# Last w_out group of a token block: the order of the products over the accumulators, and two engines that copy them out

## The chip, the cores and the metric

One core of one Trainium2 chip runs the program. The metric is device time in microseconds, as the median of several executions. A separate execution was recorded by the hardware profiler, and every row below comes from that one.

## The reference

Attention within clusters, followed by two feed-forward layers. For each of 2 batches and 8 heads (768 positions, head size 64), queries and keys are assigned to the nearest of 16 centroids, and a query attends only to keys of its own cluster. The 1536 tokens of 512 features then pass two layers of the same form:

```python
def _moe_ref(x, w_in, w_out):            # first layer, SiLU
    h = x @ w_in
    g = h * (1.0 / (1.0 + np.exp(-h)))
    return (g @ w_out).astype(np.float32)

def _moe2_ref(x, w_in, w_out, alpha):    # second layer, PReLU
    h = x @ w_in
    g = np.maximum(h, 0.0) + alpha * np.minimum(h, 0.0)
    return (g @ w_out).astype(np.float32)
```

`w_in` is 512 x 2048, `w_out` 2048 x 512. Weights arrive as 8-byte floats and are converted on the chip.

## The kernel before

All matrices are kept as two float16 parts (a high part and the rest), so that a product takes three TensorE matmuls. Attention goes over 12 token tiles of 128 and 8 heads (96 units): scores (lines 796 and 800), a VectorE scaling with minimum (810), the exponential on ScalarE (815), the two parts (819, 820), a transposing DMA (826) and the product with the values (838). Beside it the weights are loaded (892) and converted (903 to 930), and tiles that are done pass the first layer (w_in products on line 1195, w_out products on line 1226).

The second layer goes over 3 token blocks of 512 tokens (`j` = 0 to 2). A block has 4 feature groups of 4 x 128 features. For a group, `plain_in` (block 0, products on line 1415) or `wino_in` (blocks 1 and 2, a Strassen-Winograd form, products on line 1439) makes the activations `g`, with VectorE on lines 1388 to 1400 and 1448 to 1450. `layer2_out` then multiplies them with `w_out` (line 1482) and adds into four PSUM accumulators of 128 x 512 float32, one for each tile of 128 tokens. The four are the halves of two PSUM tiles, and the tile names in the traces and orders below are those of these two:

```python
bank_s = [ps.tile([128, 2, 512], F32, tag=f"s{i}", name=f"s{i}") for i in range(2)]
acc = [bank_s[t // 2][:, t % 2] for t in range(4)]
```

Tiles t = 0 and 1 are in `s0` (also written `s_64`), tiles 2 and 3 in `s1` (`s_65`). After the last group of a block ScalarE copies the four out with a scale (line 1496), and SyncE's queue sends each to the output (line 1498).

The order in which instructions stand on each engine is not the order in which the code issues them. `plan_order` at the end takes all instructions, with dependencies that it works out for itself, and schedules them by list scheduling under costs written into the class `Plan`. In these dependencies a PSUM tile counts as one cell, and two reads of one PSUM tile by different instructions are kept in order as well. It does this once in program order and 60 times with priorities from the previous result plus noise, and keeps the one whose modelled end is earliest:

```python
noise = Random(4)
found = [self.run(list(range(len(self.ins))))]
for _ in range(rounds):
    back.run([noise.gauss(0, 0.1) - t for t in self.ended])
    found.append(self.run([noise.gauss(0, 0.1) - t for t in back.ended]))
return min(found, key=lambda x: x[0])
```

The noise is drawn instruction by instruction, in program order. Each engine runs its instructions strictly in the order that comes out, and the tile framework puts in the semaphore waits.

Of the kernel before, what the change touches and what calls it, by code (L numbers as in the profile page):

```python
# [11 lines left out]
F32 = mybir.dt.float32  # L12
# [4 lines left out]
ACTF = mybir.ActivationFunctionType  # L17
ALU = mybir.AluOpType
# [311 lines left out]
def cluster_attention_silu_prelu(  # L330
# [20 lines left out]
    nc = tc.nc  # L351
    B, H, S, D = q.shape
    C = centroids.shape[1]
    DM, DFF = w1_in.shape
    T = S // 128
# [5 lines left out]
    N2 = NTILE * 128 // NC2  # L361
# [7 lines left out]
    KB = 1024  # L369
# [7 lines left out]
    def view(off, dt, *dims):  # L377
        n = 1
        for d in dims:
            n *= d  # L380
        nb = n * (2 if dt in (F16, BF16) else 4)
        assert off % 4 == 0 and nb % 4 == 0 and off + nb <= total, (off, nb)
        a = arena[:, off // 4:(off + nb) // 4]
        if dt != F32:
            a = a.bitcast(dt)
        if len(dims) == 1:
            return a
        names = [f"a{i}" for i in range(len(dims))]
        pat = f"p ({' '.join(names)}) -> p {' '.join(names)}"
        return a.rearrange(pat, **{n: d for n, d in zip(names, dims)})  # L390
# [497 lines left out]
    def out_piece(o, j):  # L888
        return view(o + 4 * KB * j, F16, 2, 2, DM)
# [377 lines left out]
    slots = [o_xt + 4 * KB * ((len(chunks) + i) % 3) for i in range(3)]  # L1267
# [109 lines left out]
    def g_buf(n):  # L1377
        return view(o_w + (32 + 8 * (n % 4)) * KB, F16, 4, 2, N2)

    def features(n):  # L1380
        j, i = groups[n]
        if j == 0:
            return [4 * i + k for k in range(4)]
        return [2 * i, 2 * i + 1, 8 + 2 * i, 9 + 2 * i]
# [87 lines left out]
    def layer2_out(n):  # L1472
        j, i = groups[n]
        first, last = i == 0, i == KF // 4 - 1
        g = g_buf(n)
        acc = [bank_s[t // 2][:, t % 2] for t in range(4)]
        for q, f in enumerate(features(n)):
            wo = out_piece(o_w, f // 2)
            for t in range(4):
                k = 0  # L1480
                for a, bb in ((0, 0), (0, 1), (1, 0)):
                    nc.tensor.matmul(  # L1482
                        out=acc[t], lhsT=g[:, q, a, t * 128:(t + 1) * 128], rhs=wo[:, bb, f % 2],
                        start=(first and q == 0 and k == 0), stop=(last and q == 3 and k == 2),
                    )
                    k += 1
        if not last:
            return
        eo = l2[:, 6 + j:7 + j]
        nc.vector.tensor_scalar(  # L1490
            eo, l2[:, 2 + j:3 + j], w2["in"].inv_smin, w2["out"].inv, op0=ALU.mult, op1=ALU.mult
        )
        nc.vector.tensor_tensor(out=eo, in0=eo, in1=l2[:, 1:2], op=ALU.mult)
        for t in range(4):
            ob = view(slots[1 + t % 2] + 2 * KB * (t // 2), F32, DM)
            nc.scalar.activation(out=ob, in_=acc[t], func=ACTF.Copy, scale=eo)
            r = j * (N2 // 128) + t
            nc.sync.dma_start(
                out=out.rearrange("(b p t) d -> b t p d", b=B, t=T)[r // T, r % T], in_=ob
            )  # L1500


    att = attention()
# [55 lines left out]
    for n in range(len(groups) + OUT_LAG):  # L1559
        if n < NG:  # L1560
            plain_in(n)
            run_bg(NPC // 2)
        elif n < len(groups):
            wino_in(n)
        if n == NG - 1:
            for w in range(2):
                wino_ops(w)
            split_x2(1)
        if n == 2 * NG - 1:
            split_x2(2)  # L1570
        if n >= OUT_LAG:
            layer2_out(n - OUT_LAG)
# [33 lines left out]
```

## Time and profile before

| what | value |
|---|---|
| median of 3 executions | 745.43 us (744.39 to 745.95) |
| the profiled execution | 744.72 us |
| its span, first to last instruction | 742.9 us |
| TensorE (PE) busy | 661.5 us, 89% of the span |
| VectorE (DVE) busy | 596.1 us, 80% |
| ScalarE (ACT) busy | 480.3 us, 65% |
| GpSimd (POOL) busy | 123.9 us, 17% |
| mean granted TensorE clock | 0.963 of full speed |

Times are microseconds from the start of the span. A busy share is an average over stages that are limited by different engines. "L1482" is line 1482 of the kernel, `s<-arena` an instruction that reads SBUF and writes PSUM tile s0 or s1 (numbers are left out), and "idle before <-X" the time that an engine stood still until X released it.

### The profile page before, as it was taken

The numbers are of one execution on the slowest core, as the hardware profiler recorded it, in microseconds if no ns is written. First come the engines' busy times: TensorE is split into PE (matmuls) and PEld (weight loads), VectorE is DVE, ScalarE is ACT, GpSimd is POOL, SyncE is SP. The second block draws the span as 40 slices with busy tenths as digits, with TensorE's granted clock in tenths as the row PEclk, the third lists the DMA queues.
The fourth block names the chain that finished last, engine by engine and source line by source line (L and its number), as shares of the span: only waits on it lengthen the run. The fifth ranks groups of instructions, "written<-read, shape, count | busy, mean of one in ns | idle before, by whom it ended". The sixth has DMA issues, their size and how long they took to land.

```text
span 742.9 us, 16966 instructions
## 1 busy us (share of the span) xinstructions
PE 661.5 (89%) x7023; PEld 500.3 (67%) x7023; DVE 596.1 (80%) x1048; ACT 480.3 (65%) x763; POOL 123.9 (17%) x231
## 2 busy tenths in 40 slices
PE   0355568799999999999999999999999999999997
PEld 0244347679988888888887888864444776666643
DVE  4799999989789479778977755979999999966640
ACT  7996877978789559667866877977773622413111
POOL 4550231211324531121220010000000000000000
PEclk9995659999999999999999999999999999999999
DMA  7989999999999897998999934343200100001001
GB/s 227 306 217 299 265 257 168 169 196 164 191 160 202 139 183 132 171 173 146 160 157 137 273 106 140 115 170 119 109 1 0 57 2 1 1 1 58 1 0 57
DMA packets 237357, 100.86 MB, mean 136 GB/s; under 512 B 217312, under 2 KB 227552, under 8 KB 237280
## 3 DMA queue, kind: packets, MB, share of 16 engines
q1 hardware_dynamic: 237280, 99.78, 62.8%
q8 instruction: 55, 0.90, 0.5%
q14 instruction: 22, 0.18, 0.1%
HBM read 43.03 MB, written 3.15 MB: 62 GB/s over the span
## 4 chain that ended last, share of the span: by engine, by line
PE 43%; DVE 13%; DMA 6%; ACT 5%; issue 4%; POOL 2%; ACTq 0%; POOLq 0%; DVEq 0%
PE s L1482 11%; PE w L1195 9%; PE w L1226 7%; PE w L1439 4%; PE x L838 3%; DVE arena L930 3%; PE m L1439 2%; PE x L1439 2%; DMA arena<-in_moe_w_out_dram 2%; PE s L800 2%; PE s L796 2%; DMA arena<-in_moe_w_in_dram 2%; DMA arena<-arena 1%; DVE arena L917 1%; DVE arena L1305 1%
## 5 line engine op out<-in xcount | busy, mean ns | idle before, releaser
L1226 PE MATMUL w<-arena 128*128 128x256 f16 (+1 forms) x1296 | 154.8, 258 | 1.2 <-ACT arena L1233 0.9
L1195 PE MATMUL w<-arena 128*128 128x256 f16 (+1 forms) x1272 | 147.6, 256 | 1.0 <-DMA arena<-arena 0.5
L1482 PE MATMUL s<-arena 128*128 128x512 f16 x576 | 132.1, 379 | 1.7 <-DVE arena L930 1.3
L838 PE MATMUL x<-arena 128*128 128x64 f16 x1728 | 117.5, 197 | 13.3 <-DMA arena<-arena 13.3
L1226 PEld LDWEIGHTS <-arena 128*128 128x128 f16 x1344 | 111.6, 99 | 14.7 <-issue 1.4
L1195 PEld LDWEIGHTS <-arena 128*128 128x128 f16 x1344 | 110.8, 98 | 14.8 <-issue 2.0
L838 PEld LDWEIGHTS <-arena 128*128 128x128 f16 x1728 | 96.5, 101 | 26.8 <-DMA arena<-arena 16.9
L810 DVE TENSOR_SCALAR_CACHE_REDUCE s<-s,stat 128x768 f32<-128x768 f32 x96 | 97.9, 1022 | 20.4 <-PE s L800 18.6
L815 ACT ACTIVATE s<-s,stat 128x768 f32<-128x768 f32 x96 | 83.9, 874 | 43.0 <-DVE s L810 41.5
L820 DVE TENSOR_TENSOR arena<-s,arena 128x768 f16<-128x768 f32 x96 | 91.4, 953 | 13.1 <-ACT arena L819 12.9
L1482 PEld LDWEIGHTS <-arena 128*128 128x128 f16 x576 | 56.1, 98 | 64.0 <-issue 2.3
L819 ACT ACTIVATE arena<-s 128x768 f16<-128x768 f32 x96 | 77.3, 809 | 1.6 <-DMA arena<-arena 0.2
L1399 ACT ACTIVATE arena<-arena,stat 128x512 f16<-128x512 f32 x48 | 33.9, 718 | 67.5 <-DVE arena L1396 67.4
L1439 PEld LDWEIGHTS <-arena 128*128 128x128 f16 x672 | 65.7, 98 | 13.6 <-DVE arena L1450 0.3
L796 PE MATMUL s<-arena 80*128 80x384 f16 x192 | 67.6, 352 | 7.2 <-DVE arena L820 5.0
L800 PE MATMUL s<-arena 128*128 128x384 f16 x192 | 67.9, 354 | 0.0
L450 POOL TENSOR_SCALAR stat<-stat 128x1 int32<-128x1 int32 (+1 forms) x41 | 10.2, 249 | 339.7 <-DVE stat L445 239.8
L930 DVE SCALAR_TENSOR_TENSOR arena<-arena,stat 128x1024 f16<-128x1024 f32 x40 | 50.9, 1289 | 8.8 <-ACT arena L929 8.8
L929 ACT ACTIVATE arena<-arena,stat 128x1024 f16<-128x1024 f32 x40 | 46.0, 1173 | 16.6 <-POOL stat L450 4.8
L914 DVE SCALAR_TENSOR_TENSOR arena<-arena 128x1024 int32<-128x1024 int32 x32 | 39.3, 1227 | 17.6 <-ACT arena L907 17.5
L1439 PE MATMUL w<-arena 128*128 128x256 f16 x336 | 52.0, 273 | 0.0
L903 ACT ACTIVATE arena<-arena 128x1024 int32<-128x1024 uint32 x32 | 36.8, 1149 | 21.9 <-DMA arena<-in_moe_w_out_dram 11.8
(176 smaller groups left out, 1036.7 us busy)
## 6 DMA issues: line engine op xcount, KB each, us to landing
arena<-in_moe_w_in_dram SPq DMA_DIRECT2D x16, 1024.0 KB, 6.3
arena<-in_moe_w_out_dram SPq DMA_DIRECT2D x16, 1024.0 KB, 5.7
arena<-in_k_dram SPq DMA_DIRECT2D x8, 384.0 KB, 4.2
arena<-in_q_dram SPq DMA_DIRECT2D x6, 512.0 KB, 5.1
arena<-in_v_dram SPq DMA_DIRECT2D x8, 384.0 KB, 5.0
out_dram<-arena SPq DMA_DIRECT2D x12, 256.0 KB, 2.1
arena<-arena SPq DMA_TRANSPOSE x149, 4.3
arena<-in_centroids_dram SPq DMA_DIRECT2D x1, 32.0 KB, 3.1
```

The lines of the kernel that those rows point to most:

```text
L796: nc.tensor.matmul(out=sc[:, j, :hs], lhsT=qt2[0:D + C, h], rhs=kt2[0:D + C, h % 2, j * hs:(j + 1) * hs], start=True, stop=False,)
L800: nc.tensor.matmul(out=sc[:, j, :hs], lhsT=qt1[:, h], rhs=kt1[:, h % 2, j * hs:(j + 1) * hs], start=False, stop=True,)
L810: nc.vector.tensor_scalar(sc[:, :, :hs], sc[:, :, :hs], nd_cols[:, H * (n % 2) + h:H * (n % 2) + h + 1], None, op0=ALU.mult, op1=ALU.min, ...
L815: nc.scalar.activation(out=p, in_=p, func=ACTF.Exp, scale=-1.0, bias=bias, accum_out=sums[n % 2][:, h:h + 1])
L819: nc.scalar.activation(out=hl[:, 0], in_=p, func=ACTF.Copy)
L820: nc.vector.tensor_tensor(out=hl[:, 1], in0=p, in1=hl[:, 0], op=ALU.subtract)
L838: nc.tensor.matmul(out=x_ps[0][:, h], lhsT=pt[:, ph * T + t], rhs=vt[:, h % 2, t, vh], start=(i == 0), stop=(i == 3 * T - 1),)
L930: nc.vector.scalar_tensor_tensor(out=lo, in0=t, scalar=s, in1=hi, op0=ALU.mult, op1=ALU.subtract)
L1195: nc.tensor.matmul(out=hp[:, ff], lhsT=wi[:, a, kd], rhs=mov(bb, kd), start=(i == 0), stop=(i == 3 * KD - 1),)
L1226: nc.tensor.matmul(out=acc, lhsT=wo[:, a, f % 2, dt * 128:(dt + 1) * 128], rhs=g[:, f, bb], start=(i == 0), stop=(i == 3 * KF - 1),)
L1439: nc.tensor.matmul(out=hp[:, ff], lhsT=a_[:, a, kd, at + 128 * ff:at + 128 * ff + 128], rhs=b_[:, bb, kd], start=(k == 0), stop=(k == 5),)
L1482: nc.tensor.matmul(out=acc[t], lhsT=g[:, q, a, t * 128:(t + 1) * 128], rhs=wo[:, bb, f % 2], start=(first and q == 0 and k == 0), stop=(la ...
```

## The change

In the last group of a token block, the code issues the products of tiles 0 and 1 for all four features first, then their copies and output DMAs, and then the same for tiles 2 and 3. VectorE copies tiles 1 and 3, ScalarE tiles 0 and 2. In the other groups the products are issued as before, through the new inner function.

```diff
-        for q, f in enumerate(features(n)):
+        def products(q, f, ts):
             wo = out_piece(o_w, f // 2)
-            for t in range(4):
+            for t in ts:
                 k = 0
                 for a, bb in ((0, 0), (0, 1), (1, 0)):
                     nc.tensor.matmul(
...
         if not last:
+            for q, f in enumerate(features(n)):
+                products(q, f, range(4))
             return
...
-        for t in range(4):
-            ob = view(slots[1 + t % 2] + 2 * KB * (t // 2), F32, DM)
-            nc.scalar.activation(out=ob, in_=acc[t], func=ACTF.Copy, scale=eo)
...
+        for ts in ((0, 1), (2, 3)):
+            for q, f in enumerate(features(n)):
+                products(q, f, ts)
+            for t in ts:
+                ob = view(slots[1 + t % 2] + 2 * KB * (t // 2), F32, DM)
+                if t % 2:
+                    nc.vector.tensor_scalar(ob, acc[t], eo, None, op0=ALU.mult)
+                else:
+                    nc.scalar.activation(out=ob, in_=acc[t], func=ACTF.Copy, scale=eo)
+                r = j * (N2 // 128) + t
+                nc.sync.dma_start(
+                    out=out.rearrange("(b p t) d -> b t p d", b=B, t=T)[r // T, r % T], in_=ob
+                )
```

In the changed file the products are line 1483, the copies line 1506 (ScalarE) and 1504 (VectorE), and the DMA line 1508. The number of instructions is the same; six copies change the engine.

The end of the program on ScalarE stood so before, with the semaphores that each instruction waits for in brackets (PE_49 is TensorE's, Activation_49 ScalarE's, DMAHW a DMA queue's):

```order
559 L1458 ACTIVATE arena<-m,stat 128x512 [waits PE_49,Activation_49]
560 L1399 ACTIVATE arena<-arena,stat 128x2x256 [waits DVE_49] x4
561 L1496 ACTIVATE arena<-s_64,stat 128x512 [waits DMAHW1_49,PE_49,Activation_49]
562 L1496 ACTIVATE arena<-s_64,stat 128x512 [waits DMAHW2_49,Activation_49]
563 L1496 ACTIVATE arena<-s_65,stat 128x512 [waits DMAHW3_49,PE_49,Activation_49]
564 L1496 ACTIVATE arena<-s_65,stat 128x512 [waits DMAHW4_49,Activation_49]
```

Two of the four copies have left ScalarE, and stand at the end of VectorE's rows, which now are these:

```order
916 L1392 SCALAR_TENSOR_TENSOR arena<-arena,stat 128x512 [waits DVE_49]
917 L1396 SCALAR_TENSOR_TENSOR arena<-arena 128x512 [waits DVE_49] x2
918 L1400 SCALAR_TENSOR_TENSOR arena<-arena,stat 128x2x256 [waits Activation_49] x3
919 L1504 TENSOR_SCALAR arena<-s_64,stat 128x512 [waits DMAHW2_49,Activation_49]
920 L1504 TENSOR_SCALAR arena<-s_65,stat 128x512 [waits DMAHW4_49,Activation_49]
```

Both new rows wait for a DMA queue and for ScalarE's semaphore, and name no wait for TensorE; the ScalarE copies of tiles 0 and 2, which stay, wait for TensorE.

On TensorE the last product into `s0` before stands five products ahead of the end (rows 14036 of 14046, every second row a weight load):

```order
14034 L1482 MATMUL s0_64<-arena_70 128x512
14035 L1482 LDWEIGHTS arena_70
14036 L1482 MATMUL s0_64<-arena_70 128x512
14037 L1482 LDWEIGHTS arena_70
14038 L1482 MATMUL s1_65<-arena_70 128x512
```

In the changed kernel it stands 22 products ahead of the end, row 14046 again being the last:

```order
14000 L1483 MATMUL s1_65<-arena_70 128x512
14001 L1483 LDWEIGHTS arena_70
14002 L1483 MATMUL s0_64<-arena_70 128x512
14003 L1483 LDWEIGHTS arena_70
14004 L1483 MATMUL s1_65<-arena_70 128x512
```

Seventeen products into `s1` more now follow the last one into `s0`.

At the end of block 0 VectorE prepares the Winograd operands (1312 to 1316 with 930) and begins block 1 (1448, 1450). Before, the place read:

```order
751 L1316 SCALAR_TENSOR_TENSOR arena<-arena,stat 128x1024
752 L930 SCALAR_TENSOR_TENSOR arena<-arena,stat 128x1024
753 L1312 SCALAR_TENSOR_TENSOR arena<-arena,stat 128x1024
754 L930 SCALAR_TENSOR_TENSOR arena<-arena,stat 128x1024
755 L1312 SCALAR_TENSOR_TENSOR arena<-arena,stat 128x1024
756 L1448 TENSOR_TENSOR arena<-w_69,arena 128x512
757 L930 SCALAR_TENSOR_TENSOR arena<-arena,stat 128x1024
758 L1450 SCALAR_TENSOR_TENSOR arena<-m,stat,arena 128x512
```

Now it reads:

```order
750 L1316 SCALAR_TENSOR_TENSOR arena<-arena,stat 128x1024
751 L1342 SCALAR_TENSOR_TENSOR arena<-arena,stat 128x512
752 L1312 SCALAR_TENSOR_TENSOR arena<-arena,stat 128x1024
753 L1504 TENSOR_SCALAR arena<-s_64,stat 128x512
754 L1504 TENSOR_SCALAR arena<-s_65,stat 128x512
755 L930 SCALAR_TENSOR_TENSOR arena<-arena,stat 128x1024
756 L1448 TENSOR_TENSOR arena<-w_69,arena 128x512
757 L930 SCALAR_TENSOR_TENSOR arena<-arena,stat 128x1024
758 L1450 SCALAR_TENSOR_TENSOR arena<-m,stat,arena 128x512
```

Block 0's two VectorE copies stand next to each other ahead of the first 1448, and the second 1312 has moved to row 779. On TensorE, the last product of block 0 into `s1` now has 17 products of line 1439 ahead of it, where it had 65.

The order also differs far from the edit. On ScalarE near the start of the program, where the first keys (608, 636, 645) and the first weights (903, 907) are prepared, the rows before were:

```order
11 L903 ACTIVATE arena<-arena 128x1024
12 L608 ACTIVATE arena<-arena,stat 128x768 x2
13 L636 ACTIVATE arena<-arena 128x12x64
14 L907 ACTIVATE arena<-arena 128x1024
15 L636 ACTIVATE arena<-arena 128x12x64
```

They are now:

```order
11 L903 ACTIVATE arena<-arena 128x1024
12 L608 ACTIVATE arena<-arena,stat 128x768
13 L907 ACTIVATE arena<-arena 128x1024
14 L636 ACTIVATE arena<-arena 128x12x64
15 L608 ACTIVATE arena<-arena,stat 128x768
```

The weight conversion 907 has moved ahead of one 608 and one 636. VectorE's rows at the same place have the conversion 914 at row 31, ahead of the first row of the first one-hot (571); before, it stood at row 34, behind three of them.

## Rows read from the trace of the kernel before

**Rows 1.** The page: the clock granted in 40 equal slices, and PE's and VectorE's busy tenths.

```profile
PE   0355568799999999999999999999999999999997
...
DVE  4799999989789479778977755979999999966640
...
PEclk9995659999999999999999999999999999999999
```

**Rows 2.** Busy time by stage; the columns follow the second line of the group.

```profile
core 0: us, PE busy (x) PEld busy (x) DVE busy (x) ACT busy (x) POOL busy (x), PEclk, DMA share, GB/s
0.00:50.00 50.00, 13.70 (x174) 10.68 (x175) 34.81 (x86) 42.79 (x65) 25.90 (x59) 1.00 0.94 264
50.00:125.00 75.00, 46.74 (x536) 34.51 (x535) 69.76 (x136) 53.93 (x75) 15.79 (x24) 0.66 1.06 247
125.00:175.00 50.00, 44.16 (x776) 39.02 (x774) 44.75 (x78) 41.89 (x73) 11.83 (x20) 0.97 0.99 173
175.00:525.00 350.00, 345.89 (x4235) 288.45 (x4232) 278.78 (x511) 264.36 (x440) 68.88 (x123) 1.00 0.81 163
525.00:575.00 50.00, 47.98 (x235) 22.32 (x234) 50.00 (x61) 29.42 (x41) 1.12 (x4) 1.00 0.02 6
575.00:650.00 75.00, 74.93 (x551) 53.41 (x550) 74.71 (x117) 30.35 (x47) 0.34 (x2) 1.00 0.04 15
650.00:725.00 75.00, 75.00 (x473) 46.18 (x472) 43.26 (x67) 15.10 (x22) 0.00 (x0) 1.00 0.04 15
725.00:743.00 18.00, 13.12 (x61) 5.77 (x59) 0.00 (x0) 2.42 (x4) 0.00 (x0) 0.99 0.16 59
```

**Rows 3.** What PE waited for up to 165 us: total us, times, longest.

```profile
PE w L950 <- DVE arena L917: 18.9, 9, 5.6
PE x L838 <- DMA arena<-arena: 12.5, 8, 3.2
...
PE s L503 <- ACT arena L651: 7.0, 2, 6.3
```

**Rows 4.** The chain that ended last, three pieces of it: start, us, what.

```profile
592.77 1.75 PE w L1439 x16
...
735.97 2.17 PE s L1482 x10
...
738.29 0.69 ACT arena L1496
```

**Rows 5.** Instructions in order of time, 736.5 us to the end.

```profile
737.13 2.42 ACT L1496 ACTIVATE arena<-s,stat 128x512 f32<-128x512 f32 x4 [22.87 <-PE s L1482]
737.85 2.07 SPq L1498 DMA_DIRECT2D out_dram<-arena  x4
```

**Rows 6.** Lines 1496 and 1498: ns min/median/max, first and last start; DMA landing.

```profile
L1496 ACT ACTIVATE arena<-s,stat x12: 668/681/697, 582.9 to 738.9; 128x512 f32<-128x512 f32 x12
...
L1498 SPq DMA_DIRECT2D out_dram<-arena x12: 332/332/360, 583.6 to 739.6; - x12
...
DMA to landing us min/median/max: 2.0/2.1/2.3
```

**Rows 7.** Line 1388: VectorE reads 512 float32 columns of PSUM with a pointer scalar.

```profile
L1388 DVE TENSOR_SCALAR arena<-w,stat x8: 735/742/746, 499.7 to 544.2; 128x512 f32<-128x512 f32 x8
```

**Rows 8.** Instructions from 712 us: VectorE's 1400 takes over from ScalarE's 1399.

```profile
713.54 0.72 ACT L1399 ACTIVATE arena<-arena,stat 128x512 f16<-128x512 f32 x1 [2.45 <-DVE arena L1396]
714.29 0.75 DVE L1400 SCALAR_TENSOR_TENSOR arena<-arena,stat 128x512 f16<-128x512 f32 x1 [0.79 <-ACT arena L1399]
```

**Rows 9.** The end of block 0 on VectorE and ScalarE, in order of time.

```profile
579.87 0.74 DVE L1342 SCALAR_TENSOR_TENSOR arena<-arena,stat 128x512 f16<-128x512 f32 x1
...
582.92 1.28 DVE L1312 SCALAR_TENSOR_TENSOR arena<-arena,stat 128x1024 f32<-128x1024 f32 x1
...
586.51 0.68 DVE L1448 TENSOR_TENSOR arena<-w,arena 128x512 f32<-128x512 f32 x1
...
589.80 0.67 ACT L1496 ACTIVATE arena<-s,stat 128x512 f32<-128x512 f32 x1
```

More of the change, by code (lines that the diff above doesn't have):

```diff
@@ L1493, in layer2_out @@
         nc.vector.tensor_tensor(out=eo, in0=eo, in1=l2[:, 1:2], op=ALU.mult)
-        for t in range(4):
-            ob = view(slots[1 + t % 2] + 2 * KB * (t // 2), F32, DM)
-            nc.scalar.activation(out=ob, in_=acc[t], func=ACTF.Copy, scale=eo)
[L1497 to L1500, printed above, removed]
+        for ts in ((0, 1), (2, 3)):
[11 more added lines that the diff above has]
+                )
     att = attention()
```

## The prediction, made before the changed kernel had run

> **What bounds the kernel now.** I began with the page's busy tenths [rows 1]: PE stands at 9 from the eighth slice to the last but one, so from about 150 us on TensorE sets the pace. VectorE is at 9 in many slices too, so the question for each stage is who waits. The busy time by stage [rows 2] says it in us. Up to 175 us PE is busy 13.70 + 46.74 + 44.16 = 104.6 us and idle 70.4 us, and in the middle of that its granted clock is 0.66 on average, a mixture of the levels of 1.2 and 2.4 GHz. From 175 to 725 us it idles 4.11 + 2.02 + 0.07 + 0 = 6.2 us, at full clock. So the time is three parts: a start in which PE waits for conversions and transposes [rows 3], 550 us in which it hardly waits, and a tail. Of the tail, the chain that ended last [rows 4] shows that the last w_out product ends at 735.97 + 2.17 = 738.14 us; the remaining 4.8 us of the span are copies, the output DMA and the program's end.
>
> What can move the time is therefore the tail, a new wait of PE after 175 us, and anything that happens in the start.
>
> **The order of the products: 0 us.** In the planner's own dependencies a PSUM tile is one cell. Products into `s0` are a chain in the order of issue, feature by feature over tiles 0 and 1, and those into `s1` another. The new loops issue each chain in the same order as before; only their mixing in the program changes, and that mixing the planner chose freely before as well. The trace has it: the first copy starts at 737.13 us [rows 5], about 1.0 us ahead of the end of the last product, which is five products at 2.17 / 10 = 0.22 us each [rows 4], as many as the old order puts behind the last one into `s0`. Now 22 are behind it, so the copies of tiles 0 and 1 start some 4.8 us ahead of the end, but they were not what the end waited for: what ends last is `s1`. The number and kind of products stay.
>
> **The tail: +0.17 us.** Before, ScalarE copies tile 2 from 738.29 us [rows 4], and tile 3 starts at 738.9 us and takes 0.68 us [rows 6]: done at 739.58, last DMA issued at 739.6. The two copies overlap by a little, as start to start is 0.6 us. After, ScalarE copies tile 2 from 738.29 to 738.98. The new order shows VectorE's copy of tile 3 waiting for ScalarE's semaphore and naming none of TensorE: I read this as a wait for the ScalarE copy out of the same PSUM tile, so that the two do not run side by side. The hand-over costs 714.29 − (713.54 + 0.72) = 0.03 us [rows 8]; a VectorE read of 512 float32 columns of PSUM with a pointer scalar takes 0.74 us [rows 7]. So it ends at 738.98 + 0.03 + 0.74 = 739.75, and its DMA goes out at 739.77, 0.17 us later than before. Two DMAs instead of four are then near the end; landing takes 2.0 to 2.3 us [rows 6], so at best 0.3 us comes back. I take none: the last landing is that of one DMA either way. Bounds: −0.13 and +0.17 us.
>
> At this place a rule speaks against my reading. The Trainium skill, "PSUM — Partial Sum Buffer", section Specifications (TRN2), says that ScalarE and VectorE can read PSUM in parallel at full bandwidth where they are not in the same bank; tiles 2 and 3 are 2 KiB per partition each, thus two of its banks. By that rule nothing in the chip keeps the copies apart. No run here shows two such reads together yet, and the wait is one that the program makes.
>
> **The ends of blocks 0 and 1: 0 us.** VectorE gets two copies of 0.74 us in each. At block 1's end PE is busy 75.00 of 75 us and VectorE only 43.26 [rows 2], so 1.5 us vanish in its slack. At block 0's end VectorE has no slack: 74.71 of 75 us [rows 2]. There the old order has six instructions from 1342 to the first 1448, 579.87 to 586.51 us, 6.64 us [rows 9]. The new order takes out a 1312 and the 930 that follows (1.20 us each, by the pitch of 582.92 to 586.51, which is three such) and puts in two copies: 6.64 − 2.40 + 1.48 = 5.72 us, and the first 1448 could come 0.9 us early. Against this stands the wait of the second copy. It needs ScalarE's copy of tile 2, which started at 589.80 before [rows 9]. On TensorE the last `s1` product has moved ahead of 48 Winograd products of 1.75 / 16 = 0.11 us [rows 4], so it can start at about 584.6 and end at 585.2. VectorE wants its second copy after 1342, 1316, 1312 and the first copy, at about 579.87 + 0.66 + 2.40 + 0.66 = 583.6. So it stands for up to 1.6 us, and the first 1448 comes between 0.9 us early and 0.7 us late. Behind it in VectorE's queue are 930 and 1450, for whose PSUM tile PE's next products wait. What hides it is PE's other work: from 575 to 650 us PE idles 0.07 us with VectorE full. Without that cover it is +0.7 us. I take 0.
>
> **The order elsewhere: 0 us, with wide bounds.** The noise is drawn in program order, and the program order has changed; the rows of the start show that another of the 61 orders has won. This touches 70.4 us of idle PE in the start and 6.2 us later. Both orders are the best of 61 under the same rules, so neither sign is preferred. As bounds I take the largest single wait of PE, 6.3 us [rows 3], gained or lost; for the likeliest case, within 1.5 us.
>
> **Sum.** 744.72 (profiled execution: span 742.9 and 1.8 around it) + 0 + 0.17 + 0 + 0 = 744.9 us. The profiled execution lies 0.71 us below the median of the runs, so against the median it is 745.43 + 0.17 = 745.6 us. A measurement of this kernel tells about 0.2% (1.5 us) from no change.
>
> **Rivals.**
>
> *Copies side by side.* If VectorE's wait is for an earlier instruction of ScalarE, the copy of tile 3 starts with that of tile 2 at 738.29 and ends at 739.03, 0.55 us earlier: 744.9 us. For it: the two halves are separate, by the rule above. Against: no wait for TensorE is named, and without the detour over ScalarE there would have to be one. No verdict hangs on it; it counts as no change.
>
> *The new order starts layer one sooner (faster).* The counted rows of the start show conversion (907, 914) ahead of key and one-hot work. PE waits 18.9 us for 917, conversion's last step, up to 5.6 us at a time, and 12.5 us for transposes, up to 3.2 us [rows 3]. If conversion comes a step sooner (one 917 of those nine waits, on average 2.1 us) and the products that it frees cover a transposing wait of 3.2 us, some 4 us are gained, allowing for overlap: 741.6 us. It decides from the point where PE's idle time before 175 us falls under 69 us.
>
> *The conversion delays the first attention units (slower).* The same rows read the other way. 914 ahead of the first 571 puts off the one-hot, its transpose, the first scores, and everything behind them in VectorE's queue, which is busy 69.76 of 75 us between 50 and 125 us [rows 2] and cannot catch up. And PE stands strictly in order: the wait of 6.3 us for 651 [rows 3] shows what one badly placed product costs. One more wait of half that size, 3.2 us, gives 748.8 us. It decides from the point where that idle time exceeds 72 us, or the clock stays at the lower level through more of 50 to 125 us: at 0.66 PE is busy 46.74 us there, at full clock the same work is 31 us, so a tenth more of this stage at the lower level is 1.5 to 2 us where PE is the one waited for.
>
> *VectorE falls behind at block 0's end (slower).* Priced above: +0.7 us, with the tail +0.9 us, 746.3 us. Alone it stays within 1.5 us; it matters only beside the rival before.
>
> **How the numbers follow.** Change without a measurable effect (my forecast, with side-by-side copies and block 0's delay in it): 0.40. Order faster by more than 1.5 us: 0.29. Order slower by more than 1.5 us: 0.31; a little over the faster one, as both direct terms are losses. The likeliest time is 745.6 us, its own range 744.1 to 747.1. The two outer cases reach 745.4 ∓ 6.3 us at the bounds; cutting a tenth off each side leaves 741.0 to 750.0.
>
> **What would show it.** Tail: VectorE's 1504 at the end begins 0.03 us after ScalarE's last 1506 has ended, and not with it; the last DMA is issued 1.6 us after the last product (now 739.6 − 738.14 = 1.5). Order of products: the first 1506 of block 2 starts some 4.8 us ahead of the last product, with nothing gained. Block 0: VectorE idle up to 1.6 us ahead of its second 1504, PE idle under 0.7 us more from 575 to 650. Order elsewhere: the difference in time, less 0.2 us, is that of PE's idle time up to 175 us and, by less, from 175 to 575. I am wrong if the tail shrinks by over 0.5 us, or if PE's idle time before 175 us moves by several us.

## The result, and the profile after

The changed kernel took 749.62 us (median of 6, 748.75 to 752.98) beside 745.07 us of the kernel before (median of 6, 744.39 to 749.38). The ratio is 1.0054 with an interval of 1.0035 to 1.0073: slower by half a per cent, 4.0 us by the ratio (the two medians are 4.55 us apart). The time lies inside the range forecast; "no change that can be measured" does not hold. The profiled execution of after is one of the six; at 752.28 us it is 2.7 us above the median of its kernel, so its 7.6 us of longer span (750.5 against 742.9) are more than the runs lost.

The page of after, the rows that answer to [rows 1]:

```profile
PE   0354567799899999999999998999999999999997
...
DVE  5799999978689589869976856779999999976640
...
PEclk9995558999999999999999999999999999999999
```

Two of TensorE's slices from the eleventh on stand at 8 where it had 9. Its busy time by stage, columns as in [rows 2]:

```profile
0.00:50.00 50.00, 13.21 (x163) 10.12 (x164) 34.53 (x85) 42.34 (x64) 26.27 (x55) 1.00 0.93 264
50.00:125.00 75.00, 48.97 (x580) 37.48 (x577) 70.29 (x134) 55.60 (x77) 14.87 (x28) 0.64 1.03 249
125.00:175.00 50.00, 43.47 (x760) 38.14 (x758) 44.57 (x79) 39.91 (x69) 11.86 (x19) 1.00 0.93 168
175.00:525.00 350.00, 341.34 (x4187) 285.25 (x4185) 268.58 (x500) 258.00 (x435) 70.85 (x124) 1.00 0.79 158
525.00:575.00 50.00, 47.83 (x230) 21.51 (x229) 49.69 (x62) 32.73 (x45) 1.31 (x4) 1.00 0.12 43
575.00:650.00 75.00, 74.34 (x529) 51.16 (x528) 75.00 (x110) 29.81 (x45) 0.78 (x2) 1.00 0.04 15
650.00:725.00 75.00, 74.87 (x499) 48.58 (x497) 54.01 (x88) 16.36 (x24) 0.00 (x0) 1.00 0.04 15
```

Up to 175 us PE is now busy 105.65 us and idle 69.35, 1.05 us less than before [rows 2]. From 175 to 525 us it is idle 350 − 341.34 = 8.66 us where it was 4.11, and from 575 to 650 us 0.66 where it was 0.07. What it waits for from 165 us on (total us, times, longest):

```profile
PE x L838 <- DMA arena<-arena: 3.3, 3, 2.0
PE s L503 <- ACT arena L944: 2.0, 4, 1.1
PE m L1195 <- DMA arena<-arena: 1.7, 1, 1.7
PE w L1226 <- ACT arena L1233: 0.9, 1, 0.9
PE m L1415 <- ACT arena L1233: 0.7, 1, 0.7
...
PE w L1439 <- DVE arena L1448: 0.7, 1, 0.7
```

No wait there is long. L838 waits for a transposing DMA of attention, L503 (a weight's sum of squares) for its conversion, L1195 for the transposed token tile, L1226 and L1415 for an eviction on ScalarE (L1233).

The tail answers to [rows 4, 5]. Two pieces of the chain that ended last, and then the instructions in order of time from 741 us:

```profile
734.79 11.24 PE s L1483 x52
...
746.10 0.70 ACT arena L1506
```

```profile
741.36 0.69 ACT L1506 ACTIVATE arena<-s,stat 128x512 f32<-128x512 f32 x1 [20.70 <-issue]
742.07 5.87 SPq L1508 DMA_DIRECT2D out_dram<-arena  x4
742.08 0.75 DVE L1504 TENSOR_SCALAR arena<-s,stat 128x512 f32<-128x512 f32 x1 [20.20 <-ACT arena L1506]
746.10 0.69 ACT L1506 ACTIVATE arena<-s,stat 128x512 f32<-128x512 f32 x1 [4.06 <-PE s L1483]
746.82 0.75 DVE L1504 TENSOR_SCALAR arena<-s,stat 128x512 f32<-128x512 f32 x1 [4.00 <-ACT arena L1506]
```

The last product ends at 734.79 + 11.24 = 746.03 us. VectorE's copy begins at 746.82, 0.03 us after ScalarE's has ended (746.10 + 0.69), and what released it was ScalarE. The line of the output DMAs, and their landing, for [rows 6]:

```profile
L1508 SPq DMA_DIRECT2D out_dram<-arena x12: 332/332/360, 585.8 to 747.6; - x12
...
DMA to landing us min/median/max: 2.0/2.0/2.1
```

### The profile page after: what moved, and what is told of

The parts are those of the page before. It is cut to its first block, busy times and chain, and to the rows that moved or that the text cites. A ratio compares the mean times of both kernels' runs of the same rounds, so it can differ in the third digit from the quotient of the medians.

```text
span 750.5 us, 16974 instructions
## 1 busy us (share of the span) xinstructions
PE 665.1 (89%) x7023; PEld 501.5 (67%) x7023; DVE 598.2 (80%) x1054; ACT 476.1 (63%) x757; POOL 125.9 (17%) x231
## 5 line engine op out<-in xcount | busy, mean ns | idle before, releaser
L1226 PE MATMUL w<-arena 128*128 128x256 f16 (+1 forms) x1296 | 148.5, 259 | 0.9 <-ACT arena L1233 0.9
L1195 PE MATMUL w<-arena 128*128 128x256 f16 (+1 forms) x1272 | 147.6, 257 | 0.7 <-DVE arena L1203 0.6
L1226 PEld LDWEIGHTS <-arena 128*128 128x128 f16 x1344 | 112.0, 99 | 13.8 <-issue 1.4
L838 PE MATMUL x<-arena 128*128 128x64 f16 x1728 | 110.6, 197 | 11.5 <-DMA arena<-arena 11.3
L1195 PEld LDWEIGHTS <-arena 128*128 128x128 f16 x1344 | 110.5, 98 | 15.0 <-issue 3.0
L838 PEld LDWEIGHTS <-arena 128*128 128x128 f16 x1728 | 92.2, 100 | 24.2 <-DMA arena<-arena 14.5
L1483 PEld LDWEIGHTS <-arena 128*128 128x128 f16 x576 | 56.1, 98 | 62.8 <-issue 0.7
L1439 PEld LDWEIGHTS <-arena 128*128 128x128 f16 x672 | 65.5, 98 | 14.4 <-issue 1.1
L450 POOL TENSOR_SCALAR stat<-stat 128x1 int32<-128x1 int32 (+1 forms) x41 | 12.5, 309 | 319.9 <-DVE stat L445 230.2
L930 DVE SCALAR_TENSOR_TENSOR arena<-arena,stat 128x1024 f16<-128x1024 f32 x40 | 51.6, 1305 | 7.6 <-ACT arena L929 7.5
L929 ACT ACTIVATE arena<-arena,stat 128x1024 f16<-128x1024 f32 x40 | 46.3, 1176 | 13.1 <-POOL stat L450 4.1
L1439 PE MATMUL w<-arena 128*128 128x256 f16 x336 | 49.5, 273 | 0.7 <-DVE arena L1448 0.7
```

The costliest lines, as they stand in the source:

```text
L838: nc.tensor.matmul(out=x_ps[0][:, h], lhsT=pt[:, ph * T + t], rhs=vt[:, h % 2, t, vh], start=(i == 0), stop=(i == 3 * T - 1),)
L930: nc.vector.scalar_tensor_tensor(out=lo, in0=t, scalar=s, in1=hi, op0=ALU.mult, op1=ALU.subtract)
L1195: nc.tensor.matmul(out=hp[:, ff], lhsT=wi[:, a, kd], rhs=mov(bb, kd), start=(i == 0), stop=(i == 3 * KD - 1),)
L1226: nc.tensor.matmul(out=acc, lhsT=wo[:, a, f % 2, dt * 128:(dt + 1) * 128], rhs=g[:, f, bb], start=(i == 0), stop=(i == 3 * KF - 1),)
L1439: nc.tensor.matmul(out=hp[:, ff], lhsT=a_[:, a, kd, at + 128 * ff:at + 128 * ff + 128], rhs=b_[:, bb, kd], start=(k == 0), stop=(k == 5),)
L1483: nc.tensor.matmul(out=acc[t], lhsT=g[:, q, a, t * 128:(t + 1) * 128], rhs=wo[:, bb, f % 2], start=(first and q == 0 and k == 0), stop=(la ...
```

## The experiments

All were timed beside runs of the kernel before on their own chip (its medians there were 747.69, 746.9 and 748.0 us), so a ratio is to be read within its batch. In kernels that change code above them, line numbers stand some 5 to 20 higher than in the kernel before. Expectations given in us go by the first batch, in which the kernel before took 745.07 us. "The old order" is that of the kernel before, "the new order" that of the changed kernel.

**Order or edit: four kernels.** In e1_old_order the planner is shown the program before (all copies priced as ScalarE's); after planning, the odd copies run on VectorE:

```diff
+            if t % 2:
+                moved.add(nc.vector.tensor_scalar(ob, acc[t], eo, None, op0=ALU.mult).ins.name)
+            else:
+                nc.scalar.activation(out=ob, in_=acc[t], func=ACTF.Copy, scale=eo)
...
+            if i.name in planned_as:
+                self.eng[n], self.cost[n], self.port[n] = 2, (0.19 + 512 / 1205.0 + 0.09,), False
```

> The planner is shown the old program (all copies as ScalarE's, old product loops), so that every engine keeps the old order; then the copies of tiles 1 and 3 are put on VectorE at the place where the plan had them begin. Theory 'order' (the 4.5 us come from the order that the planner chose for the changed program, not from the edit's own instructions): within 0.2% of before, 744.5 to 746.5 us. Rival 'edit' (VectorE's copies and their waits cost it, wherever the rest stands): near the changed kernel, 748.5 to 750 us.

Measured: 748.65 us, ratio 1.001 (0.999 to 1.003), so the edit in the old order can't be told from nothing. e2_new_order is the reverse: planned as the changed program, odd copies on ScalarE.

> The mirror: the planner is shown the changed program, so that every engine keeps the new order, and the copies of tiles 1 and 3 then run on ScalarE. Theory 'order': still as slow as the changed kernel, 748.5 to 750 us. Rival 'edit': back to 744.5 to 746.5 us.

Measured: 750.44 us, 1.0028 (1.0013 to 1.0044): the new order alone, with not one copy on VectorE, makes the kernel slower. It is half of the change's 1.0054, and less than this expectation gave (748.5 us is 1.0046 of 745.07); the interval overlaps a little with the change's (1.0035 to 1.0073). e3_loops has the new loops and all copies on ScalarE, e4_copies the old loops and odd copies on VectorE; e3_loops against the changed kernel:

```diff
-                if t % 2:
-                    nc.vector.tensor_scalar(ob, acc[t], eo, None, op0=ALU.mult)
-                else:
-                    nc.scalar.activation(out=ob, in_=acc[t], func=ACTF.Copy, scale=eo)
+                nc.scalar.activation(out=ob, in_=acc[t], func=ACTF.Copy, scale=eo)
```

> Only the product loops of the change, all copies on ScalarE. The order that the planner gives is almost the old one (1% of the rows of VectorE and ScalarE differ, around the ends of the blocks). Theory 'order': 744.5 to 746.5 us. Rival 'loops' (products tile by tile take PE's spare work away at the ends of blocks): 746.5 to 750 us.

> Only the VectorE copies of the change, product loops as before. The planner gives a third order, different from both. Theory 'order': any time of a spread of some us around the two known, 742 to 752 us, and with a lag that grows in stages that have no copies in them. Rival 'edit': 748.5 to 750 us, with the loss at the ends of the blocks.

Measured: e3_loops 746.97 us, 0.9992 (0.9976 to 1.0009); e4_copies 747.70 us, 0.9997 (0.9981 to 1.0014). The loops alone leave the order almost as it was. Of TensorE's 7,023 products, compared place by place with the kernel before, 22 come from another line of the program, against 2,774 with the whole change (691 of them up to 175 us, 1,992 from there to 525 us, 91 behind) and 3,012 with the copies alone. So what let another of the 61 orders win is the copies' move to VectorE, and the order that wins there with the old loops costs nothing.

**Where in the order: three kernels.** The changed kernel's instructions are planned twice, as the loops alone (old order) and as they are (new order), and the two are joined on every engine at one planned time, 500 us here and 210 us in new_start. In the traces TensorE's rows go over to the other order at about 518 and 219 us; the expectations say 512 and 223, which were estimates:

```diff
+    order = [
+        [n for n in x if begun[n] < 500.0] + [n for n in y if begun[n] >= 500.0]
+        for x, y in zip(one, two)
+    ]
```

> The changed kernel's instructions, in two orders joined: on every engine the old order (planned with all copies as ScalarE's, as in the kernel with the loops alone) up to the end of layer one, some 512 us, and the new order behind it. Theory (the new order loses its time in layer one, from 175 to 525 us, where TensorE stood 8.5 to 9.7 us in its four traces and 4.1 to 6.7 us in the old order's): at most 1.001 of before, TensorE idle 4 to 7 us from 175 to 525 us, and only the 0.7 us wait at the end of block 0 left. Rival (the loss lies in layer two and its copies): 1.003 to 1.006.

> The reverse: the new order on every engine up to some 512 us, the old one behind it. Theory (layer one): 1.003 to 1.006 of before, TensorE idle 8 to 10 us from 175 to 525 us and stopped near 455 us again. Rival (layer two): within 0.2% of before.

> The new order only up to some 223 us, the old one behind it. If the stop of 2 us near 195 us (L838 waits for a transposing DMA) is a part of the loss: 1.001 to 1.004 of before. If the loss of layer one lies behind it, at 375 to 520 us (weights and the last token tile late): within 0.2% of before, or a little faster, since the new order's start up to 175 us stood 1 us less.

Measured: old_then_new 748.05 us, 0.9999 (0.9982 to 1.0017); new_then_old 754.74 us, 1.0088 (1.0062 to 1.0114); new_start 747.95 us, 0.9994 (0.9972 to 1.0017). So the loss needs the new order between some 219 and 518 us, in layer one: with the old order there nothing is lost, and the new order only ahead of it costs nothing that can be measured. Behind the seam the two orders hardly differ on TensorE (the 91 products above). PE's waits from 375 to 650 us, first in old_then_new and then in new_then_old, show what goes and what stays:

```profile
PE w L1242 <- ACT arena L1249: 2.4, 1, 2.4
PE w L1455 <- DVE arena L1464: 0.7, 1, 0.7
```

```profile
PE m L1211 <- DMA arena<-arena: 2.5, 1, 2.5
PE s L518 <- ACT arena L960: 2.3, 2, 1.4
PE w L1431 <- DVE arena L1412: 2.0, 2, 1.5
```

With the old order up to the seam the waits for the token tile (L1195, here L1211) and the weight's sum of squares (L503, here L518) shrink to 0.5 us or vanish, while block 0's wait of 0.7 us for L1448 (here L1464) stays. The third row of new_then_old is new: those 2.0 us, at 524 and 528.7 us, are behind the seam, so I put about that much of its 1.0088 (above the 1.003 to 1.006 expected) down to the seam; no run shows it.

PE's idle time, window less busy, over all traces, with the time of the traced execution:

| kernel | order in layer one | traced execution | idle, 175 to 525 us | of it 375 to 525 us |
|---|---|---|---|---|
| before | old | 744.72 | 4.11 | 2.35 |
| e6_head_late | old, one product moved | 744.39 | 4.47 | 3.63 |
| e1_old_order | old | 751.98 | 5.96 | 3.91 |
| e3_loops | old | 748.15 | 6.65 | 4.23 |
| old_then_new | old | 748.23 | 5.67 | 3.05 |
| new_start | new to 219 us, then old | 750.69 | 6.93 | 4.26 |
| e4_copies | a third one | 747.76 | 5.83 | 5.51 |
| after | new | 752.28 | 8.66 | 5.57 |
| after_again | new | 756.91 | 9.68 | 6.75 |
| e2_new_order | new | 753.94 | 9.09 | 7.89 |
| e5_head_first | new, one tile moved | 751.91 | 8.54 | 7.48 |
| new_then_old | new | 753.85 | 8.70 | 7.71 |
| seed5 | another draw | 755.36 | 7.65 | 6.47 |
| seed6 | another draw | 757.93 | 11.40 | 8.53 |

The five with the old order in layer one average 5.37 us, the five with the new one 8.93 us, 3.6 us more. But these executions differ by more than the runs: they took 747.5 and 753.8 us on average, 6.3 us apart, since the traced ones of the new order lie 2.3 us above the medians of their kernels (the old ones 0.3 us). And idle time in layer one is not all that an order can lose: seed5 is 8 us slower than before with 3.5 us more of it.

**One late tile: three kernels.** after_again is the changed kernel once more.

> The changed kernel once more, beside the kernel before on this chip. Theory (the new order of the whole program costs the time): about 1.004 of before, inside 1.0035 to 1.0073, and its trace again shows TensorE standing for the transposing DMA of the last token tile ahead of the m products at L1195 near 455 us, 1.7 to 2.6 us, where the trace of before has no wait. Rival (the loss is a matter of single executions, in which a pause is or is not followed by a stretch at the lower clock): within 1.002 of before, and no wait near 455 us.

Measured: 751.75 us, 1.0074 (1.0046 to 1.0102), just above the range expected, with a stop of 2.1 us for the transposing DMA ahead of L1195. Where that stop comes from is seen by laying before and after side by side (instructions in order of time, before first):

```profile
436.34 1.20 ACT L929 ACTIVATE arena<-arena,stat 128x1024 f16<-128x1024 f32 x1
...
438.88 1.85 SPq L892 DMA_DIRECT2D arena<-in_moe_w_in_dram  x2
...
441.77 0.19 PE L838 MATMUL x<-arena 128*128 128x64 f16 x1
...
444.69 1.23 SPq L869 DMA_TRANSPOSE arena<-arena  x1
...
450.99 1.14 PE L1195 MATMUL m<-arena 128*128 128x256 f16 x9
...
451.97 0.19 PE L503 MATMUL s<-stat,arena 128*128 128x1 bf16 x2
```

```profile
444.36 1.22 ACT L929 ACTIVATE arena<-arena,stat 128x1024 f16<-128x1024 f32 x1 [3.01 <-POOL stat L450]
...
446.38 0.19 PE L838 MATMUL x<-arena 128*128 128x64 f16 x1
...
446.92 2.16 SPq L892 DMA_DIRECT2D arena<-in_moe_w_in_dram  x2
...
450.43 1.24 SPq L869 DMA_TRANSPOSE arena<-arena  x1
...
456.96 2.56 PE L1195 MATMUL m<-arena 128*128 128x256 f16 x22 [1.74 <-DMA arena<-arena]
...
459.70 0.19 PE L503 MATMUL s<-stat,arena 128*128 128x1 bf16 x2 [0.18 <-ACT arena L944]
```

The last attention products (L838) end the last token tile, which goes through VectorE and GpSimd to a transposing DMA (L869), and PE wants it at L1195. Before, that DMA is issued 5.8 us after two weight loads (L892) and PE never waits. After, loads and DMA are 3.5 us apart, and PE starts on the tile 6.5 us after the DMA's issue (450.43 to 456.96). The reader should also see the second chain: from the split of a weight piece on ScalarE (L929; when VectorE's L930 behind it has ended, the next load is issued) to the sum of squares of that next piece on PE (L503) it is 15.6 us before and 15.3 us after. Before, PE gets there without a wait.

e5_head_first lets the tile come sooner in the changed kernel:

```diff
+    pe[first - 40:first - 40] = head
...
+    dve.insert(at - 2, x)
...
+    sp.insert(at - 2, dma)
```

> The changed kernel in its own order, but the last 11 L838 products of the last token tile stand 40 products of L1226 (some 4.4 us) earlier on TensorE, VectorE's product of that tile two places earlier and its transposing DMA ahead of the two weight loads. Theory (the new order loses its time mostly where that tile comes late): no wait for the DMA ahead of L1195 near 455 us, and 2 to 3 us less than the changed kernel of the same batch, so about 1.001 of before. Rival (the loss is spread over the whole order, or is at the end of block 0): the wait goes and the time stays within 0.7 us of the changed kernel.

Measured: 750.68 us, 1.0053 (1.0035 to 1.0071), 1.07 us under after_again; the intervals overlap, so this decides for neither. The trace says more (order of time, this kernel's lines):

```profile
437.72 0.48 PE L855 MATMUL x<-arena 128*128 128x64 f16 x11
...
442.17 1.23 ACT L948 ACTIVATE arena<-arena,stat 128x1024 f16<-128x1024 f32 x1 [3.01 <-POOL stat L466]
...
444.11 1.23 SPq L888 DMA_TRANSPOSE arena<-arena  x1
445.43 1.32 SPq L911 DMA_DIRECT2D arena<-in_moe_w_in_dram  x2
...
452.56 2.56 PE L1214 MATMUL m<-arena 128*128 128x256 f16 x22
...
457.39 0.19 PE L519 MATMUL s<-stat,arena 128*128 128x1 bf16 x2 [2.27 <-ACT arena L963]
```

The wait for the tile is gone, and 4.8 us on PE stands 2.27 us for the weight piece instead. From the split (L948) to that sum of squares it is 15.2 us, as in after. Two chains were late by about as much, and shortening one uncovered the other.

e6_head_late moves a single instruction of the kernel before, the very last L838 product, 30 places back:

```diff
+    pe, n = order[0], place_of[last["products"][-1]]
+    at = pe.index(n)
+    pe.remove(n)
+    pe.insert(at + 30, n)
```

> The kernel before in its own order, but the very last L838 product stands 30 products of L1226 (some 3.3 us) later on TensorE; nothing else moves. Theory (that one tile's lateness is a price by itself): TensorE stands 1.1 to 3.5 us for the transposing DMA ahead of L1195 near 451 us, since the DMA landed at most some 2 us ahead of need in the trace of before; 1.0015 to 1.005 of before. Rival (later stages swallow such a wait, because VectorE sets the pace from 525 to 650 us): the wait is there and the time is within 0.2% of before.

```profile
443.14 0.19 PE L844 MATMUL x<-arena 128*128 128x64 f16 x1
...
446.93 1.23 SPq L877 DMA_TRANSPOSE arena<-arena  x1
...
450.02 1.14 PE L1203 MATMUL m<-arena 128*128 128x256 f16 x9 [0.77 <-DMA arena<-arena]
```

Measured: 747.04 us, 1.0003 (0.9986 to 1.002). The wait is 0.77 us, under the 1.1 to 3.5 us expected, and too small to settle anything by its time. But with the two loads issued 9.9 us earlier (436.99) the same transposing DMA needed 3.1 us from issue to PE's start (446.93 to 450.02), half of the 6.5 us in after. The other traces bear out that this goes with the place of the loads. The transposing DMA's time from issue to landing, by the time since the issue of the first of the two loads:

| issued | traces | landing after |
|---|---|---|
| 3.5 us behind the loads | after, after_again, e2_new_order, new_then_old | 6.5, 6.8, 7.3, 7.3 us |
| 3.8 us | e4_copies | 6.0 us |
| 5.8 us | before, e1_old_order, e3_loops, old_then_new | 4.4, 3.8, 4.2, 4.0 us |
| 9.9 us | e6_head_late | 3.0 us |
| 1.3 us ahead of them | e5_head_first | 3.0 us |

e5_head_first is the new order with this DMA moved ahead of the loads, and there it lands in 3.0 us. So in the new order the tile is late twice over: its products come later, and its DMA falls among the weight loads.

**Other draws: two kernels.** The kernel before with `Random(5)` and `Random(6)` in place of `Random(4)`:

```diff
-        noise = Random(4)
+        noise = Random(5)
```

> The kernel before with another seed for the noise of the planner's 60 further orders, nothing else changed. Theory (which order wins is as good as drawn, and orders differ by some tenths of a per cent): 0.995 to 1.010 of before, and nothing about it follows from the change. Rival (the planner's best orders are alike on the chip): within 0.2% of before.

> The kernel before with a third seed of the planner's noise. Theory (the winner of 61 orders is a draw on the chip): 0.996 to 1.011 of before, as likely slower than faster, and away from 1 by more than 0.2%. Rival (the first other seed was an exception): within 0.2% of before.

Measured: 754.96 us, 1.011 (1.0088 to 1.0132), and 756.27 us, 1.0117 (1.0087 to 1.0146). Two other draws, with nothing changed in the program, cost twice what the change cost. Both lie just above the ranges expected (1.010 and 1.011).

## Why the prediction was right or wrong

**The order of the products: right.** The first copy of block 2 starts at 741.36 us, 4.7 us ahead of the last product's end, and nothing is gained by it. With the loops alone the ratio is 0.9992 (0.9976 to 1.0009).

**The tail: right in its mechanism, small in both directions.** The copies out of one PSUM tile go one after the other, with the hand-over of 0.03 us that was forecast. The last DMA is issued 1.57 us after the last product (747.6 − 746.03; before 1.46), +0.11 for the +0.17 forecast. The span, though, ends 4.47 us after that product (750.5 − 746.03) instead of 4.76: 0.29 us are won at the end of the program, where I had taken none and allowed 0.13. This gain is the loops' and not the copies': the span ends 4.5 us after the last product in all eight traces with the new loops, two of which have every copy on ScalarE (e2_new_order, e3_loops), and 4.8 us after it in e1_old_order and e4_copies, which have VectorE's copies in the old loops. The rival with copies side by side falls. By the Trainium skill, "PSUM — Partial Sum Buffer", section Specifications (TRN2), different banks can be read by the two engines in parallel; the trace names a wait of the program (4.00 us, for ScalarE's L1506), and whether the chip would have read both banks at once no run here shows.

**The end of block 0: its price right, its cover not.** VectorE does not stand ahead of its second copy. ScalarE's copy of tile 2 has just ended when VectorE comes to its two copies (in order of time):

```profile
590.65 1.28 DVE L1312 SCALAR_TENSOR_TENSOR arena<-arena,stat 128x1024 f32<-128x1024 f32 x1
591.16 0.67 ACT L1506 ACTIVATE arena<-s,stat 128x512 f32<-128x512 f32 x1
591.84 1.40 DVE L1504 TENSOR_SCALAR arena<-s,stat 128x512 f32<-128x512 f32 x2
...
594.36 0.68 DVE L1448 TENSOR_TENSOR arena<-w,arena 128x512 f32<-128x512 f32 x1
...
595.09 1.91 PE L1439 MATMUL w<-arena 128*128 128x256 f16 x16 [0.66 <-DVE arena L1448]
```

VectorE is full (75.00 of 75 us), the two copies stand ahead of L1448, and PE stops 0.66 us for it. I had taken 0 because PE had other work; the upper bound of 0.7 us was about the value. That the copies are the cause, the other traces show: from 575 to 725 us PE is idle 0.00 to 0.15 us in the four with the old or new order and all copies on ScalarE (before, e2_new_order, e3_loops, e6_head_late), and 0.79 to 1.14 us in the eight with copies on VectorE. e2_new_order, which differs from the changed kernel in the copies' engine alone, has none of it. So the edit has a price of its own, some 0.7 to 1.1 us less the 0.3 us at the end, too small for the runs to show. Another order can lose as much there without it: seed6, with all copies on ScalarE, is idle 1.34 us. At block 1's end, where I had also taken 0, next to nothing shows (75 − 74.87 = 0.13 us from 650 to 725 us).

**The order elsewhere: the step that failed.** Of the sum's terms this one was mis-sized: 0 us where the order costs most of the 4.0 us. I took 0 with "neither sign is preferred", placed the uncertainty in the start ("up to 175 us and, by less, from 175 to 575"), and gave as reason that the noise is drawn in an order that had changed. Each part needs mending. The place: the start gained 1.05 us of idle time, and with the new start alone the ratio is 0.9994; the loss is in layer one, where before had only 4.11 us of idle time and the new order has 8.5 to 9.7. The cause: not the new program order (the loops alone keep the old winner), but the engine of the copies. The sign: of four redrawn orders three are slower (1.0028 to 1.0074 for the new one, 1.011, 1.0117) and one is the same (0.9997); none is faster. Four draws are few, and why the old order should be a good one no run shows. The bound of 6.3 us, the largest single wait, was wide enough for the change but not for the two seeds (8.1 and 8.3 us). And my signs of being wrong were blind to this loss: the tail shrank by 0.29 us and the idle time before 175 us moved by 1.05 us.

That the time lies in the range is in part luck. 749.62 us is 0.4 us inside its upper end, and the repeat's 1.0074 would be 750.9 us on 745.43, outside it. "Slower by more than 1.5 us" came with a chance of 0.31, but for a loss in the start.

The two rivals about the start fall with it: idle time before 175 us is 69.35 us, between the 69 and the 72 us from which they were to decide, and the new start alone costs and gains nothing that can be measured (0.9994, 0.9972 to 1.0017). The slower rival's clock was there in the trace (granted clock 0.64 from 50 to 125 us, a mixture of the two levels, beside 0.66 before), but PE's idle time moved the other way, by 1.05 us.

**The size.** 3.6 us more idle time in layer one, 0.66 us at block 0 and −0.29 us at the end make 4.0 us, as much as the ratio says (1.0054 of 745.07). That they meet is a coincidence: the first is a mean of executions that lie 6.3 us apart, the others come from one execution each. What is shown is that most of the loss is in layer one, and that block 0's end adds some 0.7 to 1.1 us.

What stays open: how the 3.6 us divide between the last token tile, the weight pieces and the evictions on ScalarE. e5_head_first shows only that the second stands behind the first. Moving the evictions at L1233 ahead of the conversions that they follow was not tried.

## What to carry to other kernels

Where a search under modelled costs sets the order of all instructions, an edit in one place can redraw the whole, and the draw can outweigh the edit: here the edit in the old order cost 0.1% (not to be told from nothing), the new order without the moved copies 0.3%, both together 0.5 to 0.7%, and another seed 1.1%. So first plan the new program under the old costs and run that, to see the edit alone; only then look at what the new order does. And look for the loss not only in the stage with the most idle time: here it was in one where TensorE had run 345.89 of 350 us. Two chains beside it were long enough there to stop it when they came some microseconds later, and shortening one showed the other.

## What the runs showed of the hardware

**The same order scatters by several us.** Runs of e1_old_order spread from 746.14 to 751.98 us, and those of the kernel before beside them from 744.75 to 751.05. One wait of layer one was 0.85 us in before, 2.38 in old_then_new, 3.08 in e3_loops and 3.66 in e1_old_order, all at one place of nearly one order (e1_old_order, order of time):

```profile
487.99 1.10 ACT L912 ACTIVATE arena<-arena 128x1024 int32<-128x1024 uint32 x1 [2.76 <-DMA arena<-in_moe_w_out_dram]
...
489.99 0.46 ACT L1242 ACTIVATE arena<-w,stat 128x256 f32<-128x256 f32 x1
490.49 1.87 PE L1235 MATMUL w<-arena 128*128 128x256 f16 x8 [3.66 <-ACT arena L1242]
```

A 0.46 us eviction stands on ScalarE behind a conversion that itself stood 2.76 us for a weight load, and PE stands for the eviction. "PSUM — Partial Sum Buffer" of the Trainium skill, section Engine vs sequencer instructions, says that ScalarE's queue is strictly first in, first out, and the trace agrees: what ScalarE evicts at 489.99 us comes only after the conversion of 487.99 us. That conversion stood 0.50, 1.81, 2.28 and 2.76 us for the weight load in these four traces, in the order of the waits above: the load's arrival differs, and through ScalarE's queue PE inherits it.

**Some stops go with a stretch at the lower clock.** In the same trace of e1_old_order PE stands until 490.49 us. The mean granted clock is 0.57 from 489 to 497 us, a mixture of the two levels, and 1.00 from 475 to 489 and from 497 to 525 us. The same place in new_start, with a stop of 2.60 us until 490.12 us, has 1.00 throughout. At the late token tile the clock is 0.66 from 459 to 464 us in after_again, behind a stop of 2.07 us that ended at 458.77, and 1.00 from 452 to 465 us in new_then_old, with a stop of 2.54 us that ended at 453.58. So some stops go with a stretch at the lower level, and others that are as long do not; that a stop brings it about is read from this, not tried.

**The granted clock of a trace can miss a stretch at the lower level.** From 60 to 80 us the view gives 1.00 for seed5 and 0.50 for before, yet a product of 128 x 384 (line 800) takes 527 ns on average in both. So the clocks of the start (0.64 and 0.66 above) are to be checked against the duration of a product before two kernels are compared by them.
